# A gated linear attention kernel with a feed-forward layer: order of the constants, padded first keys and queries, a new planner table

## The chip, the cores and the metric

The kernel runs on one core of a Trainium2 chip. The metric is the device time of one execution in microseconds (us). One core has five engines with a queue of instructions each: PE (TensorE: matmuls, with weight loads beside them), ACT (ScalarE), DVE (VectorE), POOL (GpSimd) and SP (SyncE, which here only issues DMA transfers). Each engine works through its queue strictly in order; an instruction that waits holds all that stand behind it on that engine.

## The reference

Gated linear attention over 4 batches, 8 heads, 768 tokens and head dimension 48, then one feed-forward layer over the 3072 tokens with 384 features and 2048 hidden features:

```python
for t in range(S):                       # S = 768
    state = alpha[:, :, t, :, None] * state + einsum('bhd,bhe->bhde', k[:, :, t], v[:, :, t])
    y[:, :, t] = einsum('bhd,bhde->bhe', q[:, :, t], state)
x = y.transpose(0, 2, 1, 3).reshape(3072, 384)
h = x @ w_in                             # 384 x 2048
g = where(h >= 1, h, where(h <= -1, 0, (h + 1) ** 2 / 4))
out = g @ w_out                          # 2048 x 384
```

## The kernel before

**Tiles.** The tokens are cut into 24 chunks j of 128 tokens (one batch, all eight heads each, four chunks to a step in time). Three chunks make a group of 384 tokens, and the feed-forward layer runs group by group (eight groups), each over 16 steps f of 128 hidden features.

**Attention.** `prepare(j)` loads a chunk's alpha (`raw_a`, L448), keys and queries (`raw_kq`, two transfers of 48 rows, L452), values (`vt`, L464) and values again by half chunks (`both`, two transfers of 64 rows, L472). `raw_a`, `raw_kq` and `both` have two buffers that chunks use in turn, and `vt` two as well, so a load waits until the chunk two before it is done with the buffer. DVE then runs a scan (L489), a reciprocal (L493), a second scan (L496) and the multiplications of keys (L504) and queries (L521). PE transposes the keys (L541), ACT copies them (L544), PE makes scores (L556) and the state's update (L569), and `follow` masks the scores (DVE L670; for early chunks a part by ACT L642 and POOL L652), makes the shifted copy of the queries (`other`: ACT L634, or a DMA for late chunks), and grows the state (ACT L609 for the first chunk of a batch, DVE L615, L707) and places it (ACT L597, or a DMA for j >= BYDMA). PE multiplies out the chunk (L731), and `end_chunk` writes it into `xs`: for group 0 one ACT copy (L759), for later groups an ACT copy (L765), a DVE subtraction (L770) that leaves the low part, and, after a group's last chunk, six SP transfers within `xs` (L786).

**Feed-forward layer.** `hidden` multiplies x by w_in (L835 for group 0, whole fp32; L844 for the others, three products of high and low parts), ACT and DVE apply the activation (L875 twice, L885), for the split groups ACT and DVE cut the result in high and low parts (L894, L895), and `second` multiplies by w_out (L917 for group 0, L926 for the others). The products of `hidden` go to two PSUM buffers, which DVE's L885 sets free.

**Weights.** They arrive as 64-bit words, eight blocks u each of w_in and w_out (L420, 768 KB a transfer), and `decode` makes fp32 of them: ACT L344 and L352, DVE L360, L371 and L383. Group 0 takes the decoded weights; for the groups behind it `part_w` makes the high part (ACT L389), the negated high part (ACT L392), and the low part by a POOL transfer that adds the weights to it (L397). The buffers of the weights (`wt`) are shared by raw words and parts.

**Order.** A planner in Python (`Plan.order`) puts all these into one order for all engines before the kernel is built. Every operation has a cost in us and a key (a due time); at each step the planner takes the engine that can start first, and on it, among the operations that could start within NEAR of the first, the one with the lowest key. The numbers of the table at L29 to L52 shift these keys: FETCH, FETCH0 and LOAD say how long ahead of use weights and chunks are fetched, DECODE and DECODE0 how long ahead weights are decoded, PARTED when the parts are made, MARGIN and its kin how far attention runs ahead of the layer that uses it; MERGE says from which chunk PE takes update, scores and the preceding chunk's outputs in one `burst`; HELP up to which chunk ACT and POOL take masks; BYSUM, BYDMA as above and in the change. Where the planner sees PE idle before WARMTH us it adds products of zeros (`fill`, L977).

**Ends.** Before the plan stand constants (L244 to L273). After it, PE, DVE and SP add up a flag (L1006 to L1021), and every engine branches on it around `stepwise`, a slow fallback that these inputs do not need. In names of the rows below a number behind a name is a buffer's.

Of the kernel before, what the change touches and what calls it, by code (L numbers as in the profile page):

```python
# [8 lines left out]
F32 = mybir.dt.float32  # L9
# [32 lines left out]
AHEAD = 20  # L42
FIRST = 3
ROOM = 2
LATER = 4.5
MERGE = 4
WARMTH = 110
HELP = 9
BYSUM = 0
LATE = 9.5  # L50
BYDMA = 14
NEAR = 0  # L52
# [23 lines left out]
class Plan:  # L76
# [23 lines left out]
    def op(self, engine, us, key, emit, reads=(), writes=(), port=False, mode=None, moved=0, after=(), beside=False, other=None, ends=None):  # L100
        o = Op(engine, us, key, emit, port, mode, moved)
        o.ends = ends or mode
# [31 lines left out]
    def order(self):  # L134
        free = {"PE": 1.1, "DVE": 3.2, "ACT": 2.2, "POOL": 5.0, "SP": 0.8}
# [15 lines left out]
        while any(ready.values()):  # L151
# [48 lines left out]
            if o.moved > 0:  # L200
                wire = max(wire, t) + o.moved / self.RATE
                t = max(wire, t + self.LAND)
            else:
                t += self.HOP.get(o.engine, 0.08)
# [26 lines left out]
def gated_attention_ffn(ctx: ExitStack, tc: tile.TileContext, q, k, v, alpha, w_in, w_out, by, out):  # L231
# [12 lines left out]
    zeros = const.tile([P, P], BF16, name="zeros")  # L244
    nc.vector.memset(zeros, 0.0)
    nothing = zeros[:, None, :].broadcast_to([P, 2, P])
    ST = CH + 1
    raw_a = const.tile([P, 2, G * ST + 1], F32, name="raw_a")
    raw_kq = const.tile([P, 2, 2, G, CH], F32, name="raw_kq")
    for i in range(2):  # L250
        nc.vector.memset(raw_kq[:, i], 0.0)
    fwd = const.tile([P, G, ST], F32, name="fwd")
    nc.gpsimd.memset(fwd, FLOOR)
    nc.gpsimd.memset(fwd[:, :, 0], 1.0)  # L254
    bwd = const.tile([P, G, ST], F32, name="bwd")
    nc.gpsimd.memset(bwd, FLOOR_INV)
    ident = const.tile([P, P], F32, name="ident")
    make_identity(nc, ident)

    mask = const.tile([P, P], F32, name="mask")  # L260
    nc.gpsimd.memset(mask, 1.0)
    nc.gpsimd.affine_select(
        out=mask, in_=mask, compare_op=ALU.is_ge, fill=0.0, base=0, pattern=[[1, P]], channel_multiplier=-1
    )

    HC = CH // 2
    both = const.tile([P, 2, 2, 2, G, 64], F32, name="both")
    for i in range(2):
        nc.gpsimd.memset(both[:, i], 0.0)
    half_b = const.tile([P, 1], F32, name="half_b")  # L270
    nc.gpsimd.memset(half_b, 0.5)
# [922 lines left out]
```

## Time and profile before

| | |
|---|---|
| device time, median of 3 runs | 516.04 us (515.94 to 517.14) |
| the profiled execution | 516.63 us |
| its span (first to last record) | 514.7 us |
| PE, DVE, ACT, POOL busy, share of the span | 97%, 65%, 60%, 7% |
| chain that ended last, PE's share | 84% |

The profiled execution has 1.93 us outside its span and lies 0.59 us above the median. Times in rows are us from the span's start. PE is nearly always busy. The places where it waits, or works on fills, are the first 32 us (the attention of the first chunks), a handover near 100 us from group 0 to group 1, and the last 6 us.

### The profile page before, as it was taken

How to read it: one execution, taken by the hardware profiler on the slowest of the kernel's cores; microseconds unless marked ns; L12 is line 12 of the kernel's file. 1: busy time of each engine (PE TensorE's matmuls, PEld its weight loads, DVE VectorE, ACT ScalarE, POOL GpSimd, SP SyncE). 2: the span in 40 equal slices, each digit the busy share in tenths (PEclk: the TensorE clock that was granted, in tenths of full speed). 3: DMA queues.
4: the chain of work that ended last, by engine and by line, in shares of the span. 5: the costliest groups of instructions: out<-in, count | busy, mean ns of one | idle time of the engine just before them, and what ended most of it. 6: DMA issues, size and time to landing. Idle time of an engine off the chain costs nothing.

```text
span 514.7 us, 11495 instructions
## 1 busy us (share of the span) xinstructions
PE 498.7 (97%) x4685; PEld 457.8 (89%) x4685; DVE 334.2 (65%) x590; ACT 307.2 (60%) x573; POOL 37.2 (7%) x71
## 2 busy tenths in 40 slices
PE   7889999989999999999999999999999999999995
PEld 5765656579999999999999999999999999999994
DVE  7889998877557847667467667487656545343332
ACT  2879988879965655655453554453553554555551
POOL 6200011222200000000000000000000000000000
PEclk9999999999999999999999999999999999999998
DMA  8999976798634303233123423145123200000001
GB/s 236 288 358 331 268 181 139 156 211 180 126 86 111 114 22 89 74 83 96 43 67 85 138 68 91 56 101 152 35 55 67 96 19 15 16 14 34 1 2 52
DMA packets 33757, 56.08 MB, mean 109 GB/s; under 512 B 12352, under 2 KB 20512, under 8 KB 33696
## 3 DMA queue, kind: packets, MB, share of 16 engines
q1 hardware_dynamic: 31392, 48.97, 34.1%
q0 software_dynamic: 2304, 6.29, 6.8%
q8 instruction: 39, 0.64, 0.5%
q14 instruction: 22, 0.18, 0.1%
HBM read 39.38 MB, written 4.72 MB: 86 GB/s over the span
## 4 chain that ended last, share of the span: by engine, by line
PE 84%; ACT 4%; DMA 4%; issue 3%; DVE 2%; POOL 1%; SPq 1%; POOLq 0%
PE ps L926 35%; PE ps L844 34%; PE ps L731 5%; DMA wt<-wt 3%; PE ps L569 2%; PE ps L556 2%; PE ps L835 2%; PE ps L541 2%; PE ps L917 1%; PE ps L977 1%; DMA xs<-xs 1%; ACT wt L352 1%; ACT gf L875 1%; ACT w L344 1%; SPq L786 1%
## 5 line engine op out<-in xcount | busy, mean ns | idle before, releaser
L844 PE MATMUL ps<-xs,wt 128*128 128x384 f32 x1008 | 194.0, 337 | 2.2 <-DMA xs<-xs 2.2
L926 PE MATMUL ps<-gh,wt 128*128 128x384 f32 x1008 | 195.9, 340 | 0.0
L844 PEld LDWEIGHTS ps<-xs,wt 128*128 128x128 f32 x1008 | 175.9, 188 | 4.1 <-issue 2.7
L926 PEld LDWEIGHTS ps<-gh,wt 128*128 128x128 f32 x1008 | 177.1, 188 | 0.6 <-issue 0.2
L885 DVE SCALAR_TENSOR_TENSOR gf<-gf,ps 128x384 f32<-128x384 f32 x128 | 70.3, 550 | 87.7 <-ACT gf L875 87.0
L875 ACT ACTIVATE gf<-ps,half_b 128x384 f32<-128x384 f32 x128 | 74.3, 580 | 77.8 <-PE ps L844 76.3
L894 ACT CAST gh<-gf 128x384 fp32r<-128x384 f32 x112 | 57.2, 512 | 73.6 <-DVE gf L885 57.8
L895 DVE TENSOR_TENSOR gh<-gf,gh 128x384 fp32r<-128x384 f32 x112 | 62.0, 555 | 48.8 <-ACT gh L894 48.2
L875 ACT ACTIVATE gf<-gf 128x384 f32<-128x384 f32 x128 | 67.3, 526 | 3.6
L917 PE MATMUL ps<-gf,wt 128*128 128x384 f32 x96 | 33.1, 489 | 1.0 <-DVE gf L885 1.0
L835 PE MATMUL ps<-xs,wt 128*128 128x384 f32 x96 | 33.1, 489 | 0.0
L496 DVE TENSOR_TENSOR_SCAN inv<-raw_a,bwd 128x516 f32<-128x516 f32 x24 | 29.6, 1232 | 2.1
L489 DVE TENSOR_TENSOR_SCAN pre<-raw_a,fwd 128x516 f32<-128x516 f32 x24 | 29.6, 1232 | 1.7 <-POOL fwd L254 1.5
L512 POOL COPY meet<-inv 128x4 f32<-128x4 f32 x24 | 11.5, 480 | 262.2 <-DVE inv L496 262.2
L917 PEld LDWEIGHTS ps<-gf,wt 128*128 128x128 f32 x96 | 17.9, 190 | 13.4 <-DVE gf L885 1.7
L835 PEld LDWEIGHTS ps<-xs,wt 128*128 128x128 f32 x96 | 17.8, 190 | 11.3
L670 DVE TENSOR_TENSOR Q<-ps,mask 64x256 f32<-64x256 f32 x48 | 20.3, 423 | 11.2 <-DMA other<-Q 6.0
L731 PE MATMUL ps<-other,both 128*64 128x64 f32 x372 | 26.8, 225 | 0.0
L731 PE MATMUL ps<-Q,both 128*64 128x64 f32 x372 | 26.8, 225 | 0.0
L731 PEld LDWEIGHTS ps<-Q,both 128*64 128x64 f32 x372 | 23.5, 138 | 2.6 <-DVE w L360 0.5
L731 PEld LDWEIGHTS ps<-other,both 128*64 128x64 f32 x372 | 23.5, 138 | 0.0
L765 ACT CAST xs<-ps 128x512 fp32r<-128x512 f32 x21 | 12.3, 588 | 18.6 <-PE ps L731 18.4
(61 smaller groups left out, 395.0 us busy)
## 6 DMA issues: line engine op xcount, KB each, us to landing
raw_kq<-in_kq SPq DMA_DIRECT2D x48, 192.0 KB, 3.9
raw_a<-in_al SPq DMA_DIRECT2D x24, 258.5 KB, 3.4
both<-in_vb SPq DMA_DIRECT2D x48, 128.0 KB, 2.9
wt<-in_w_in SPq DMA_DIRECT2D x8, 768.0 KB, 9.2
wt<-in_w_out SPq DMA_DIRECT2D x8, 768.0 KB, 9.9
wt<-wt POOLq DMA_DIRECT2D x16, 384.0 KB, 4.9
vt<-in_vt SPq DMA_DIRECT2D x24, 192.0 KB, 3.8
out<-ot SPq DMA_DIRECT2D x24, 192.0 KB, 2.0
```

The costliest lines, as they stand in the source:

```text
L489: lambda: nc.vector.tensor_tensor_scan(flat(pre()), a[:, 0:n], flat(fwd), 0.0, ALU.mult, ALU.max),
L496: lambda: nc.vector.tensor_tensor_scan(flat(inv())[:, ::-1], a[:, 1 : n + 1][:, ::-1], flat(bwd)[:, ::-1], 0.0, ALU.mult, ALU.max),
L670: lambda r=r, u=u, to=to: nc.vector.tensor_tensor(out=to()[halves[1 - r], :, halves[u]], in0=ss(j, r)[halves[u]], in1=mask[halves[u], None ...
L731: nc.tensor.matmul(out=ps()[halves[r], to, halves[u]], lhsT=lhsT[:, u, r], rhs=x()[:, g, halves[u]], start=m + u == 0, stop=True, skip_gro ...
L835: nc.tensor.matmul(out=h(), lhsT=raw_in(f)[:, kt], rhs=whole_x(n)[:, kt].rearrange("p j t -> p (j t)"), start=kt == 0, stop=kt == KT - 1,)
L844: nc.tensor.matmul(out=h(), lhsT=win(f, w)[:, kt], rhs=xs[n]()[:, 0 : groups[n], kt, a], start=(m == 0), stop=(m == 3 * KT - 1),)
L875: lambda: nc.scalar.activation(out=gf(), in_=in_(), func=func, scale=scale, bias=bias),
L885: lambda: nc.vector.scalar_tensor_tensor(out=gf(), in0=gf(), scalar=1.0, in1=h(), op0=ALU.min, op1=ALU.max),
L894: plan.op("ACT", 0.08 + 0.41 * w, key + 0.4, lambda: nc.scalar.copy(out=gh()[:, 0], in_=gf()), [gf], [gh])
L895: sub = lambda e: e.tensor_tensor(out=gh()[:, 1], in0=gf(), in1=gh()[:, 0].bitcast(F32), op=ALU.subtract)
L917: nc.tensor.matmul(out=o_ps[seg][m](), lhsT=raw_out(f)[:, m * P : (m + 1) * P], rhs=gh(), start=f == f0, stop=f == f1 - 1,)
L926: nc.tensor.matmul(out=o_ps[seg][m](), lhsT=wout(f, w)[:, m * P : (m + 1) * P], rhs=gh()[:, a], start=(f == f0 and i == 0), stop=(f == f1 ...
```

## The change

The constants are written in a fixed order (`tc.manual_schedule()`), the keys and queries of the first two chunks come as one transfer of 128 rows each with zeros for the pads (`in_kq0`, 512 KB), instead of DVE memsets and two transfers of 48 rows (192 KB each). ACT's copy of the state (L609 before, L613 after) stands behind the first two masks of its chunk and may no longer go to DVE. The planner's table has new values. The condition on BYSUM is turned round: for weight blocks u below 7 the low part comes by POOL's transfer as before, for u = 7 by a DVE subtraction. The fallback's six loops of 128 steps become one of 768, and it writes its result through another buffer.

```diff
-FETCH = 11
-LOAD = 4.5
+FETCH = 5
+LOAD = 7.5
-PARTED = 7.0
-PREPARE = 2.5
-MARGIN = 8.0
-MARGIN0 = 14.0
-MARGIN1 = 7.0
-FETCH0 = 11
-DECODE0 = 1
+PARTED = 4.5
+PREPARE = 2.0
+MARGIN = 9.0
+MARGIN0 = 15.0
+MARGIN1 = 9.0
+FETCH0 = 6
+DECODE0 = 8.0
...
-MERGE = 4
-WARMTH = 110
-HELP = 9
-BYSUM = 0
-LATE = 9.5
-BYDMA = 14
+MERGE = 3
+WARMTH = 40
+ONCE = 7.0
+SOON = 6.0
+HELP = 7
+BYSUM = 7
+LATE = 11.5
+BYDMA = 23
...
-    for i in range(2):
-        nc.vector.memset(raw_kq[:, i], 0.0)
-    nc.gpsimd.memset(fwd, FLOOR)
-    nc.gpsimd.memset(fwd[:, :, 0], 1.0)
...
+    with tc.manual_schedule():
+        nc.vector.memset(zeros, 0.0)
+        nc.vector.memset(fwd[:, :, 0:1], 1.0)
+        nc.gpsimd.memset(fwd[:, :, 1:], FLOOR)
+        nc.gpsimd.memset(bwd, FLOOR_INV)
+        make_identity(nc, ident)
+        nc.gpsimd.memset(both[:, 0], 0.0)
...
-            if u >= BYSUM:
+            if u < BYSUM:
...
+            if j < 2:
+                load(
+                    at,
+                    lambda: nc.sync.dma_start(out=raw_kq[:, i].rearrange("p x g t -> p (x g t)"), in_=kq0[j]),
...
-                    other=("DVE", 0.33, lambda: nc.vector.tensor_copy(out=state[:, b], in_=up(j, 0)), False),
+                    after=after,
...
-                    key - 0.1,
+                    key - SOON,
                     lambda: nc.sync.dma_start(out=other()[HC:], in_=Q()[HC:]),
...
-        for c in range(S // P):
-            with tc.For_i(0, P, 1) as t:
+        with tc.For_i(0, S, 1) as t:
```

Three places show how the order moves. The first is SP, from the first block of w_in on. Before (`wt_384` is the first block of w_out, `wt_158`, `wt_256` and `wt_471` are blocks of w_in, `in_al` is alpha):

```order
L420 DMA wt_158<-in_w_in 128x768
L452 DMA raw_kq_61<-in_kq 48x1024 x2
L464 DMA vt_249<-in_vt 128x384
L420 DMA wt_256<-in_w_in 128x768
L448 DMA raw_a_60<-in_al 128x517
L472 DMA both_77<-in_vb 64x512 x2
L452 DMA raw_kq_61<-in_kq 48x1024 x2
L420 DMA wt_384<-in_w_out 128x768
L464 DMA vt_461<-in_vt 128x384
L472 DMA both_77<-in_vb 64x512 x2
L420 DMA wt_471<-in_w_in 128x768
```

After (`wt_471` is the first block of w_out, `wt_377` the second of w_in; the first of w_in stands two rows ahead of this piece):

```order
L477 DMA both_65<-in_vb 64x512 x2
L450 DMA raw_kq_60<-in_kq 48x1024 x2
L469 DMA vt_346<-in_vt 128x384
L446 DMA raw_a_59<-in_al 128x517
L418 DMA wt_377<-in_w_in 128x768
L450 DMA raw_kq_60<-in_kq 48x1024
L477 DMA both_65<-in_vb 64x512 x2
L450 DMA raw_kq_60<-in_kq 48x1024
L469 DMA vt_467<-in_vt 128x384
L418 DMA wt_471<-in_w_out 128x768
```

The first block of w_out now stands behind alpha, keys, queries and values of chunk 4 (`vt_467` is chunk 4's), before it stood behind those of chunk 3 without their values.

The second place is ACT, round the first activations of group 0 (`gf`). Before (`wt_384` and `w_647` belong to the first block of w_out, whose L352 stands five rows ahead of this piece, `wt_471` to the third of w_in):

```order
L642 COPY other_583<-ps_549 64x4x64 x2
L609 COPY state_84<-ps_546 128x192
L597 COPY both_77<-state_84 48x4x48 x2
L344 ACTIVATE w_604<-wt_471 128x768
L875 ACTIVATE gf_608<-ps_586,half_b_80 128x384
L875 ACTIVATE gf_608<-gf_608 128x384
L352 ACTIVATE wt_471<-wt_471 128x768
L875 ACTIVATE gf_634<-ps_600,half_b_80 128x384
L765 CAST xs_641<-ps_615 128x4x128
L875 ACTIVATE gf_634<-gf_634 128x384
L344 ACTIVATE w_647<-wt_384 128x768
```

After (`wt_471` and `w_598` belong to the first block of w_out):

```order
L548 COPY ks_567<-ps_540 128x512
L638 COPY other_575<-Q_536 64x512
L601 COPY both_65<-state_85 48x4x48
L389 ACTIVATE wt_534<-wt_534 128x768
L341 ACTIVATE w_598<-wt_471 128x768
L349 ACTIVATE wt_471<-wt_471 128x768
L647 COPY other_575<-ps_550 64x4x64 x2
L880 ACTIVATE gf_614<-ps_570,half_b_66 128x384
L880 ACTIVATE gf_614<-gf_614 128x384
L880 ACTIVATE gf_619<-ps_603,half_b_66 128x384
L880 ACTIVATE gf_619<-gf_619 128x384
```

Both ACT steps of the first block of w_out have come to stand ahead of the first `gf`, where one of them stood behind two pairs of `gf`; the state's copy has left the place ahead of the first `gf` and now follows the second pair.

The third place is ACT at the handover from group 0 to group 1, up to the copy that writes group 1's last chunk (`xs`, from PSUM buffer 1127 before, 1125 after). Before:

```order
L392 ACTIVATE wt_1039<-wt_1039 128x768
L544 COPY ks_1086<-ps_1074 128x512
L875 ACTIVATE gf_1089<-ps_1041,half_b_80 128x384
L875 ACTIVATE gf_1089<-gf_1089 128x384
L389 CAST wt_1144<-wt_591 128x768
L392 ACTIVATE wt_1144<-wt_1144 128x768
L389 CAST wt_1150<-wt_610 128x768
L634 COPY other_1158<-Q_1066 64x512
L765 CAST xs_641<-ps_1127 128x4x128
L642 COPY other_1158<-ps_1096 64x4x64 x2
```

After:

```order
L389 ACTIVATE wt_1023<-wt_1023 128x768
L386 CAST wt_1066<-wt_622 128x768
L880 ACTIVATE gf_1079<-ps_1047,half_b_66 128x384
L548 COPY ks_1086<-ps_1074 128x512
L880 ACTIVATE gf_1079<-gf_1079 128x384
L389 ACTIVATE wt_1066<-wt_1066 128x768
L386 CAST wt_1146<-wt_655 128x768
L638 COPY other_1154<-Q_1064 64x512
L770 CAST xs_753<-ps_1125 128x4x128
L647 COPY other_1154<-ps_1094 64x4x64 x2
```

Between the copy of keys (`ks`) and the copy to `xs` stand one CAST to a part of the weights and one negation (ACTIVATE `wt`) now, where there were two CASTs and one negation.

## Rows read from the trace of the kernel before

**Rows 1.** Windows: length, busy per engine (PE, PEld, DVE, ACT, POOL), clock, DMA share, GB/s.

```profile
5.00:10.00 5.00, 3.21 (x28) 2.38 (x26) 4.90 (x8) 0.00 (x0) 2.19 (x2) 1.00 1.05 244
30.00:40.00 10.00, 9.01 (x87) 5.83 (x88) 8.23 (x15) 8.08 (x16) 0.66 (x1) 1.00 1.04 352
32.00:100.00 68.00, 68.00 (x485) 41.95 (x485) 61.80 (x95) 61.47 (x103) 9.49 (x13) 1.00 0.86 235
110.00:500.00 390.00, 390.00 (x3617) 382.25 (x3617) 234.14 (x436) 218.98 (x421) 13.43 (x26) 1.00 0.29 73
```

**Rows 2.** Chain in order of time up to 110 us: start, length, what.

```profile
23.44 0.55 PE ps L569 x21
...
29.41 1.58 issue
...
31.80 4.07 PE ps L835 x12
35.87 1.08 PE ps L731 x32
36.95 6.00 PE ps L835 x18
```

**Rows 3.** Timeline of DVE, first scan: start, length, operation, idle before and its releaser.

```profile
4.70 1.37 DVE L489 TENSOR_TENSOR_SCAN pre<-raw_a,fwd 128x516 f32<-128x516 f32 x1 [1.53 <-POOL fwd L254]
```

**Rows 4.** First block of w_out: its issue on SP, and its KB and us to landing.

```profile
18.43 0.41 SPq L420 DMA_DIRECT2D wt<-in_w_out  x1
```

```profile
wt<-in_w_out SPq DMA_DIRECT2D x1, 768.0 KB, 9.3
```

**Rows 5.** Groups by line and shape, ACT and DVE: busy, mean ns, idle before.

```profile
L344 ACT ACTIVATE w<-wt 128x768 f32<-128x768 f32 x16 | 14.6, 913 | 1.1 <-DMA wt<-in_w_in 1.1
L597 ACT COPY both<-state 48x192 f32<-48x192 f32 x48 | 16.7, 348 | 0.8
L360 DVE TENSOR_SCALAR w<-w 128x768 int32<-128x768 int32 x16 | 8.9, 554 | 0.0
L371 DVE SCALAR_TENSOR_TENSOR w<-wt,w 128x768 int32<-128x768 int32 x16 | 15.3, 958 | 0.5
L383 DVE CUSTOM_DVE_ANT_0 wt<-wt,w 128x1536 uint16<-128x1536 uint16 x16 | 15.4, 960 | 0.6
L670 DVE TENSOR_TENSOR Q<-ps,mask 64x256 f32<-64x256 f32 x48 | 20.3, 423 | 11.2 <-DMA other<-Q 6.0 <-ACT state L609 1.8 <-ACT other L634 1.4
L885 DVE SCALAR_TENSOR_TENSOR gf<-gf,ps 128x384 f32<-128x384 f32 x128 | 70.3, 550 | 87.7 <-ACT gf L875 87.0
```

**Rows 6.** Timeline of PE at the handover, from the end of a burst on.

```profile
94.52 6.07 PE L917 MATMUL ps<-gf,wt 128*128 128x384 f32 x18
101.64 1.56 PE L917 MATMUL ps<-gf,wt 128*128 128x384 f32 x4 [1.04 <-DVE gf L885]
...
106.42 0.76 PE L844 MATMUL ps<-xs,wt 128*128 128x384 f32 x3 [2.16 <-DMA xs<-xs]
```

**Rows 7.** Timeline of ACT there.

```profile
95.54 0.83 ACT L389 CAST wt<-wt 128x768 fp32r<-128x768 f32 x1 [1.21 <-DMA wt<-wt]
96.40 0.61 ACT L634 COPY other<-Q 64x512 f32<-64x512 f32 x1
97.04 0.58 ACT L765 CAST xs<-ps 128x512 fp32r<-128x512 f32 x1
```

**Rows 8.** SP's issues of the transfers within `xs`, and the chain's last of them to its landing.

```profile
98.37 3.95 SPq L786 DMA_DIRECT2D xs<-xs  x6
```

```profile
101.72 4.56 DMA xs<-xs
```

**Rows 9.** DMA issues over the whole run: KB each, median us to landing.

```profile
xs<-xs SPq DMA_DIRECT2D x42, 48.0 KB, 2.2
```

```profile
wt<-wt POOLq DMA_DIRECT2D x16, 384.0 KB, 4.9
```

**Rows 10.** Timeline of SP, last output transfers.

```profile
508.00 1.53 SPq L965 DMA_DIRECT2D out<-ot  x3
```

More of the change, by code (lines that the diff above doesn't have):

```diff
@@ L98, in pool, with op @@
         self.sizes[name] = bufs, share or name, first or bufs
-    def op(self, engine, us, key, emit, reads=(), writes=(), port=False, mode=None, moved=0, after=(), beside=False, other=None, ends=None):
+    def op(self, engine, us, key, emit, reads=(), writes=(), port=False, mode=None, moved=0, after=(), beside=False, other=None, ends=None, land=None):
         o = Op(engine, us, key, emit, port, mode, moved)
+        o.land = land or self.LAND
         o.ends = ends or mode
@@ L134, in order @@
     def order(self):
-        free = {"PE": 1.1, "DVE": 3.2, "ACT": 2.2, "POOL": 5.0, "SP": 0.8}
+        free = {"PE": 1.1, "DVE": 1.2, "ACT": 2.2, "POOL": 4.5, "SP": 0.8}
         slots = {name: [(0.0, -i, None) for i in range(n)] for name, (n, share, _) in self.sizes.items() if share == name}
@@ L268, in gated_attention_ffn @@
[L268 to L271, printed above, removed]
-    ones = const.tile([P, 1], F32, name="ones")
-    nc.gpsimd.memset(ones, 1.0)
+    ST, HC = CH + 1, CH // 2
+    one = lambda name, shape, dt=F32: const.tile(shape, dt, name=name)
+    zeros = one("zeros", [P, P], BF16)
+    raw_a = one("raw_a", [P, 2, G * ST + 1])
+    raw_kq = one("raw_kq", [P, 2, 2, G, CH])
+    fwd, bwd = one("fwd", [P, G, ST]), one("bwd", [P, G, ST])
@@ new lines, in gated_attention_ffn @@
+    ident, mask = one("ident", [P, P]), one("mask", [P, P])
+    both = one("both", [P, 2, 2, 2, G, 64])
+    half_b, ones = one("half_b", [P, 1]), one("ones", [P, 1])
+    nothing = zeros[:, None, :].broadcast_to([P, 2, P])
+    with tc.manual_schedule():
[5 more added lines that the diff above has]
+        nc.gpsimd.memset(both[:, 0], 0.0)
+        nc.gpsimd.memset(mask, 1.0)
+        nc.gpsimd.affine_select(
+            out=mask, in_=mask, compare_op=ALU.is_ge, fill=0.0, base=0, pattern=[[1, P]], channel_multiplier=-1
+        )
+        nc.gpsimd.memset(both[:, 1], 0.0)
+        nc.gpsimd.memset(half_b, 0.5)
+        nc.gpsimd.memset(ones, 1.0)
@@ new lines, in stepwise @@
+            nc.vector.tensor_tensor(out=st, in0=st, in1=cols["a"], op=ALU.mult)
+            nc.vector.tensor_tensor(out=vr, in0=vr, in1=cols["k"], op=ALU.mult)
+            nc.vector.tensor_tensor(out=st, in0=st, in1=vr, op=ALU.add)
+            nc.vector.tensor_tensor(out=vr, in0=st, in1=cols["q"], op=ALU.mult)
+            yr = sb.tile([1, BH * D], F32, name="yr")
+            for z in range(NZ):
+                y = ps.tile([1, 512], F32, name="y")
+                nc.tensor.matmul(
+                    out=y,
+                    lhsT=ones[0:D],
+                    rhs=vr.rearrange("d n e -> d (n e)")[:, z * 512 : (z + 1) * 512],
+                    start=True,
+                    stop=True,
+                )
+                nc.vector.tensor_copy(out=yr[:, z * 512 : (z + 1) * 512], in_=y)
@@ L1139, in stepwise @@
                 nc.vector.tensor_copy(out=ot[:, m], in_=o[m])
-            nc.sync.dma_start(out=out.rearrange("(m p) t -> p m t", p=P)[:, :, bass.ds(r, P)], in_=ot)
+            nc.sync.dma_start(out=whole.rearrange("(m p) t -> p m t", p=P)[:, :, bass.ds(r, P)], in_=ot)
+        for b in range(B):
+            nc.sync.dma_start(
+                out=out.rearrange("m (c b t) -> m b c t", b=B, t=P)[:, b],
+                in_=whole.rearrange("m (b c t) -> m b c t", b=B, t=P)[:, b],
+            )
 _INS = ["q", "k", "v", "alpha"]
```

109 lines of the change are left out of this document (43 added, 66 removed).

## The prediction

> **What bounds the kernel now.** I read the windows of the long middle first: from 110 to 500 us PE is busy for 390.00 of 390.00 us, ACT for 219 and DVE for 234, the granted clock is 1.00 and DMA stands at 0.29 [rows 1]. There the products are the time, and the change takes none of them away; what ACT, DVE, POOL or SP gain or lose in this stretch is hidden as long as nobody makes PE wait. Group 0's stretch, 32 to 100 us, has PE at 68.00 of 68.00 as well, but with little beside it that is free: DVE 61.80, ACT 61.47, DMA 0.86. So time can be had or lost in three places alone. I then read the chain up to 110 us: it shows when group 0's products start (L835 at 31.80, the third step's at 36.95) and what stands ahead of them [rows 2]. The timeline of PE at the handover shows two waits, 1.04 us for the activation and 2.16 us for the transfers within `xs` [rows 6]; between the end of the burst at 94.52 and the first product of group 1 that needs those transfers, at 106.42, lie 11.90 us, of which 3.20 are these waits and 8.70 are work. The last place is the tail: the last output is issued until 509.53 [rows 10], the span ends at 514.7, and 1.93 us lie outside it.
>
> **Constants, padded keys, state copy.** The first scan waits 1.53 us for POOL's memset of a column of `fwd` [rows 3]. DVE now sets this column itself and has no memsets of `raw_kq` ahead of it, so the scan can start up to 1.5 us sooner, and the first chunk's keys are not behind four 48-row transfers any more. Pads cost 256 KB in all; from the windows' 244 and 352 GB/s [rows 1] that is 0.7 to 1.1 us of wire. But a sooner first chunk pays only if group 0's products also start sooner, and those need the first block of w_in decoded, with the steps of three chunks mixed in on ACT and DVE. Before, 1.58 us of "issue" on PE itself end 0.8 us ahead of L835 [rows 2]. I put the start of the first product at about 30 us, between 29.4 (all of that issue time gone, sooner chunks) and 31.8 (nothing gained). The state copy behind the masks takes away up to 1.8 us of DVE's waits (L670 waiting for L609) [rows 5]; by itself nothing, since it is the same chain.
>
> Of the issue time, the row shows PE without work for 1.58 us while its operands wait for nothing [rows 2]. The Trainium skill, page "Runtime: NRT & Kernel Launch", section "Instruction fetch mechanics", says that crossing to the next block of an engine's instructions is "mostly hidden"; if this stall is such a crossing, the row disagrees by 1.58 us with the DMA engines at 1.04 of their share. By the rule the sum below would be the same, less a stall that could come back.
>
> **The first block of w_out.** This is the cost. Before, it is issued at 18.43 and lands 9.3 us later, at 27.7 [rows 4], well ahead of use. Now SP has it behind chunk 4's loads. The values of chunk 4 take the buffer of chunk 2, which PE's update of chunk 2 sets free; that began at 23.44 before [rows 2], and with chunks up to 1.5 us sooner I put its end at 22 to 24. So the issue is at 22.3 to 24.0, and with 9.3 us the landing at 31.6 to 33.3. A second way by bytes, from the shapes in SP's order: ahead of it stand now alpha 5 x 258.5 KB, two transfers of 512, six of 192 for keys, five of 192 for values, eight of 128 and two blocks of 768, with itself 7.8 MB in place of 6.2; 1.5 MB more at 352 or 244 GB/s [rows 1] is 4.5 to 6.3 us, so 32.2 to 34.0. Both hold the same delay, so they are not added. I take 32.0, near the first way's lower half, because the transfers now start sooner and more of them have 128 rows.
>
> What waits for it: ACT has both its decode steps of this block ahead of the first `gf`, and DVE has all three of its steps and two masks ahead of its own step of that `gf`. PE can make steps 0 and 1 of group 0, then both PSUM buffers are taken until DVE is through. From landing on that is 0.91 + 0.55 + 0.96 + 0.96 + 2 x 0.42 + 0.55 = 4.77 us [rows 5], so step 2 starts at 32.0 + 4.8 = 36.8. Before, it starts at 36.95, with 1.08 us of outputs (L731) done that now come later [rows 2]: at like work, 35.87. Loss: **+0.9 us**. Ends: without the wait PE would come to step 2 at 29.4 + 4.07 + 0.55 = 34.0, which is -1.9; with landing at 34.0 it is +2.9.
>
> **The handover.** Before, ACT stands in L389 until 95.54, waiting 1.21 us for a POOL transfer of low parts, then makes `other` (0.61), and only at 97.04 copies the burst's result to `xs` [rows 7], 2.5 us after the burst's end. Behind this stand DVE's L770, six SP issues (3.95 us from 98.37) and a landing of 4.56 [rows 8], and the `gf` for which PE waits 1.04. Now there is one CAST fewer on the way. The one that is left (L386 of `wt_1146`) waits for the transfer two ahead (of `wt_1023`), whose negation stands ahead of the keys' copy rather than of this piece's end. So the copy to `xs` begins between 0 (the CAST is held as long as before) and 2.4 us sooner (only the burst's end binds). The landing can also come down from 4.56 towards the run's median of 2.2, and the chain need only be done 8.70 us after the burst: 0.1 to 2.5 for the copy's start, 1.3 for copy and subtraction, 3.4 to the last issue, 2.2 to 4.6 for landing is 7.0 to 11.8 [rows 7 to 9]. So between all and nothing of the 3.2 us is saved. I take the copy at +0.7 and the landing at 3.4, which gives 8.8, nearly all hidden, and keep half a us for the `gf`: **-2.6 us** (0 to -3.2).
>
> **Tail and fallback.** Fewer instructions of the fallback lie to be jumped over; the nearest row to such a jump is the issue time of 1.58 [rows 2], so 0 to -1.6, and I take **-0.3**. The page and section named above say that a taken branch to code outside the loaded blocks stops for a fetch; no run here shows whether this branch is one.
>
> **Costed at nothing.** Chunks 14 to 22 lose DMA placements to ACT: nine chunks with four copies of 0.35 and one of 0.61 [rows 5, 7], 18 us of ACT between 310 and 450 us, under PE at 100%, with ACT at 56% [rows 1]. If that cover were gone, PE would wait for `gf` by single steps of 0.5 us. The last two low parts on DVE cost two steps of about 0.96 and free two ACT steps of 0.8 and two POOL transfers of 4.9 [rows 5, 7, 9], in group 1, where DVE has room. SP's earlier query transfers and three more fills (91 to 94) hold nothing that PE waits for, as far as the rows go.
>
> **Sum.** 0.9 - 2.6 - 0.3 = -2.0 on the profiled 516.63, so 514.6 there; the median lies 0.59 lower, which makes 514.0.
>
> **Rivals.** (B) The handover does not move: ACT is still held by the POOL transfer, or SP's six issues and a landing of 4.56 take the place of that wait. For it: each of SP, POOL and ACT is near full there, and DMA at 0.86 [rows 1]. Then 0.9 - 0.3 gives 516.6, no change; with some 1 us saved, 515.6. (C) **Slower**: the first block of w_out lands late. From landing on, every us is PE time; the loss is landing less 31.1. Against a saving of 2.9 it makes the kernel slower by over 0.3% (1.55 us) from a landing at 35.6, against a saving of 1.0 at the handover from 33.6, which the count by bytes reaches. At 34.5 with 1.0 saved: 3.4 - 1.0, 518.4. (D) The landing is hidden anyway: chunk 2's update comes before 21, the block lands at 30, and step 2 waits for PE alone. Then -1 at the front, -3.2 and -0.3: 511.5. (E) The edit does not do what it says: the first scan waits for alpha rather than for `fwd`, and the chunks are no sooner; the update of chunk 2 then stays at 24.0, which is the landing of 33.3 and +2.2 in place of 0.9, so 515.3.
>
> **How the numbers follow.** A measurement of this kernel can tell some 0.3% from no change, 1.55 us: faster is below 514.49, slower above 517.59. Chances: the forecast with its neighbours within 1.3 us 0.43, of which 0.31 faster and 0.12 within the bounds; D 0.17, faster; B 0.17 and E 0.07, within the bounds; C 0.16, of which all is counted slower. Faster 0.48, same 0.36, slower 0.16. The range goes from 511.2, just past D, to 517.6, which leaves most of C out above.
>
> **What would show it.** In the trace after: the first block of w_out lands at 31 to 34 us, and the third step of L840 starts within 0.3 us of that plus 4.8 (right), or PE shows no wait ahead of it (D). At the handover the copy L770 starts within 1.4 us after the burst's end, and PE waits for `xs` less than 1 us (right), or about 2 or more (B). From the handover to 500 us PE stays at 100%; a stretch with less would make the costs at nothing wrong. The time from the last issue of an output to the span's end shows the tail.

## The result

The changed kernel takes 512.27 us at the median of 10 runs (509.38 to 518.14), the kernel before beside it 516.73 (514.8 to 517.86, 10 runs): a ratio of 0.9901, 95% interval 0.9874 to 0.9928, so about 5.1 us faster (4.5 by the medians). (Ratios, here and below, leave out disturbed executions, here one of the ten; medians do not.) The prediction was 514.0 for the median, with a range from 511.2 to 517.6, and 514.6 for the profiled execution. The profiled execution took 510.89 with a span of 509.2, before 516.63 with 514.7: 5.5 us of span to explain.

Cut at two points that both kernels have, the end of group 0's burst of attention outputs (94.52 before [rows 6], 94.46 after) and the end of the last product (508.45 before, 504.78 after), they are:

| stretch | before | after | difference | forecast |
|---|---|---|---|---|
| start to end of the burst | 94.52 | 94.46 | -0.06 | +0.9 |
| burst to last product | 413.93 | 410.32 | -3.61, of it waits at the handover -3.20 | -2.6 |
| last product to end of span | 6.25 | 4.42 | -1.83 | -0.3 |

The sum has the right sign and two of its three terms came out larger, while the loss at the front did not come. All three terms erred the same way, so the profiled execution lies 3.7 us under the forecast for it.

### The profile page after: what moved, and what is told of

Read it like the earlier page. It is cut to its first block, busy times and chain, and to the rows that moved or that the text cites. A ratio compares the mean times of both kernels' runs of the same rounds, so it can differ in the third digit from the quotient of the medians.

```text
span 509.2 us, 11489 instructions
## 1 busy us (share of the span) xinstructions
PE 498.2 (98%) x4688; PEld 457.8 (90%) x4688; DVE 331.4 (65%) x584; ACT 326.3 (64%) x623; POOL 36.0 (7%) x66
## 4 chain that ended last, share of the span: by engine, by line
PE 85%; DMA 7%; ACT 4%; issue 3%; SPq 0%; POOL 0%; DVE 0%; POOLq 0%
PE ps L931 32%; PE ps L849 31%; PE ps L840 6%; PE ps L922 6%; PE ps L736 4%; DMA wt<-in_w_in 3%; PE ps L573 2%; DMA wt<-wt 2%; PE ps L560 2%; DMA vt<-in_vt 2%; PE ps L545 1%; ACT gf L880 1%; ACT wt L389 1%; ACT gh L899 1%; ACT wt L386 1%
## 5 line engine op out<-in xcount | busy, mean ns | idle before, releaser
L840 PE MATMUL ps<-xs,wt 128*128 128x384 f32 x96 | 33.3, 491 | 0.7 <-ACT xs L764 0.7
L922 PE MATMUL ps<-gf,wt 128*128 128x384 f32 x96 | 33.2, 487 | 0.0
L601 ACT COPY both<-state 48x192 f32<-48x192 f32 x84 | 29.3, 349 | 1.3
L840 PEld LDWEIGHTS ps<-xs,wt 128*128 128x128 f32 x96 | 17.7, 190 | 12.6 <-ACT xs L764 0.8
L922 PEld LDWEIGHTS ps<-gf,wt 128*128 128x128 f32 x96 | 17.9, 190 | 11.7
```

What stands on the lines that cost most here:

```text
L601: lambda r=r, to=to: nc.scalar.copy(out=to, in_=state[low[r], b]),
L840: nc.tensor.matmul(out=h(), lhsT=raw_in(f)[:, kt], rhs=whole_x(n)[:, kt].rearrange("p j t -> p (j t)"), start=kt == 0, stop=kt == KT - 1,)
L922: nc.tensor.matmul(out=o_ps[seg][m](), lhsT=raw_out(f)[:, m * P : (m + 1) * P], rhs=gh(), start=f == f0, stop=f == f1 - 1,)
```

## The profile after

The changed kernel's windows, in the columns of [rows 1]: length, busy time of PE, PEld, DVE, ACT and POOL, granted clock, DMA share, GB/s.

```profile
32.00:100.00 68.00, 68.00 (x515) 41.97 (x514) 63.30 (x97) 61.08 (x105) 9.53 (x12) 1.00 0.85 245
110.00:500.00 390.00, 389.76 (x3534) 382.64 (x3534) 231.75 (x427) 239.84 (x472) 10.99 (x22) 1.00 0.25 65
```

The long middle is as full as before: what was costed at nothing cost nothing. ACT has 21 us more in it (239.84 for 218.98), which is the 18 us of copies in chunks 14 to 22 and some more, and PE waits 0.24 us in all.

The front: DVE's first scan, PE's first update and then its rows from the first product of group 0 on, DVE's step on the first two `gf`, and the issue and landing of the first block of w_out (SP's row, then KB and us to landing).

```profile
3.60 1.23 DVE L493 TENSOR_TENSOR_SCAN pre<-raw_a,fwd 128x516 f32<-128x516 f32 x1 [2.58 <-DMA raw_a<-in_al]
```

```profile
10.48 0.68 PE L573 MATMUL ps<-vt,ks 64*64 64x48 f32 x32 [1.97 <-DMA vt<-in_vt]
...
30.89 2.20 PE L840 MATMUL ps<-xs,wt 128*128 128x384 f32 x6 [0.67 <-ACT xs L764]
33.03 0.68 PE L573 MATMUL ps<-vt,ks 64*64 64x48 f32 x32
33.64 6.07 PE L840 MATMUL ps<-xs,wt 128*128 128x384 f32 x18
39.55 2.10 PE L922 MATMUL ps<-gf,wt 128*128 128x384 f32 x6
```

```profile
38.00 1.02 DVE L890 SCALAR_TENSOR_TENSOR gf<-gf,ps 128x384 f32<-128x384 f32 x2
```

```profile
24.70 0.42 SPq L418 DMA_DIRECT2D wt<-in_w_out  x1
```

```profile
wt<-in_w_out SPq DMA_DIRECT2D x1, 768.0 KB, 8.3
```

The scan is 1.1 us sooner than in [rows 3], although it now waits for alpha, the sign that rival E named. The gain does not last: PE waits 1.97 us for the values of chunk 0, which land later (issued at 2.69 they take 7.7 us; before, issued at 1.27, they took 2.8). The first product starts at 30.89, and ends a wait for ACT's copy L764, which stands behind the decode of a block of w_in that landed at 28.0. The block of w_out lands at 24.70 + 8.3 = 33.0, and PE waits for it nowhere.

The handover, PE's rows from the burst on, then ACT, SP and POOL there, to be laid beside [rows 6 to 8]; the last row is the time from issue to landing of the six transfers.

```profile
94.46 7.36 PE L922 MATMUL ps<-gf,wt 128*128 128x384 f32 x22
101.36 3.66 PE L849 MATMUL ps<-xs,wt 128*128 128x384 f32 x18
```

```profile
94.11 0.83 ACT L386 CAST wt<-wt 128x768 fp32r<-128x768 f32 x1 [1.88 <-DMA wt<-wt]
94.96 0.62 ACT L638 COPY other<-Q 64x512 f32<-64x512 f32 x1
95.60 0.58 ACT L770 CAST xs<-ps 128x512 fp32r<-128x512 f32 x1
```

```profile
94.55 1.12 SPq L477 DMA_DIRECT2D both<-in_vb  x2
95.72 0.58 SPq L469 DMA_DIRECT2D vt<-in_vt  x1
96.94 3.96 SPq L791 DMA_DIRECT2D xs<-xs  x6
```

```profile
92.53 0.84 POOL L394 DMA_DIRECT2D wt<-wt  x1 [2.54 <-ACT wt L389]
...
100.48 0.87 POOL L394 DMA_DIRECT2D wt<-wt  x1 [2.87 <-ACT wt L389]
```

```profile
DMA to landing us min/median/max: 2.2/2.2/2.5
```

No wait is left in PE's rows. ACT's copy starts at 95.60 instead of 97.04, SP's first issue at 96.94 instead of 98.37, and the slowest landing is 2.5 instead of 4.6. POOL's transfer, which was issued before the last of the six (at 101.72 [rows 8]),

```profile
101.19 0.86 POOL L397 DMA_DIRECT2D wt<-wt  x1 [1.79 <-ACT wt L392]
```

now comes 0.2 us behind it: 100.48 to 100.3.

The tail is the chain's last pieces:

```profile
501.58 3.20 PE ps L931 x17
504.78 0.02 issue
504.80 0.56 DVE ot L322
```

From 504.78 to 509.2 are 4.42 us. In the kernel before the last product ends at 508.45,

```profile
505.25 3.20 PE ps L926 x17
```

and the span at 514.7.

## Experiments

All times are medians, the ratio is to runs of the kernel before on the same chip with its 95% interval. Two kernels come from exchanging one part (the fallback), two from doing one part alone, and eight from moving single steps in the finished order: `moved_behind(order, steps, anchor)` takes the named steps, and whatever depends on them or follows them on their engine among those held, to just behind the anchor.

**The tail: the fallback alone, and the change without it.** Kernel before with the short fallback; kernel after with the long one.

```diff
-        for c in range(S // P):
-            with tc.For_i(0, P, 1) as t:
+        with tc.For_i(0, S, 1) as t:
```

> The kernel before with the short fallback alone. Theory (tail): the fallback's length is what an engine jumps over at the end, so the time from the last product to the span's end falls from 6.25 us (before) to about 4.4 us (the whole change shows 4.42), all else is as before, and the time falls by 1.8 us, ratio 0.9965. Rival: the shorter tail comes from where the last outputs land or from where instructions lie after the reordering; then the tail stays at about 6.2 us and the ratio is 1.000.

> The changed kernel with the long fallback of before put back. Theory (tail): from the last product to the span's end about 6.2 us again, 1.8 us more than with the whole change (4.42), so about 3.6 us under the kernel before in the profile, ratio 0.993 to 0.994. Rival (tail from another part of the change): 4.4 us, ratio 0.990.

Measured: 515.1 us, 0.9961 (0.9931 to 0.999), for the short fallback alone; 514.66, 0.9914 (0.9883 to 0.9945), for the change without it. In the traces the chain of the first ends

```profile
506.78 3.20 PE ps L926 x17
509.98 0.02 issue
```

of a span of 514.5: 4.5 us to the end. In the second it ends at 503.85 of 509.9, which leaves 6.05:

```profile
500.65 3.20 PE ps L931 x17
```

The short loop takes 1.6 to 1.7 us off the end, in either kernel. All fourteen profiles of this document part the same way: from the last product to the end are 5.96 to 6.40 us in the eight kernels with the long fallback and 4.38 to 4.79 in the six with the short one. A jump over the code would explain why code that no run enters costs time there, but the runs show the size alone, not which instruction takes it.

**The rest by halves.** First the planner's numbers, the condition on BYSUM and the earlier query transfers, on the kernel before; then the constants, the padded keys and the state copy, on the kernel before.

```diff
-BYSUM = 0
+BYSUM = 7
...
-            if u >= BYSUM:
+            if u < BYSUM:
```

> The kernel before with the new table alone (with the turned condition on BYSUM, the earlier query transfers and the landing time that the planner takes for the low parts), old constants, old first loads, old fallback. Theory (the handover is the table's): PE waits under 0.5 us in all at the handover from group 0 to group 1, where before waits 1.04 + 2.16; the tail stays at 6.2 us; the first product of group 0 starts within 1 us of before (31.8). Time 2.5 to 3.5 us under before, ratio 0.993 to 0.995. Rival (the handover came from the earlier front, since PE's burst ends at the same time in both): PE still waits 2 us or more there, ratio 0.999 to 1.000.

```diff
+    with tc.manual_schedule():
+        nc.vector.memset(zeros, 0.0)
+        nc.vector.memset(fwd[:, :, 0:1], 1.0)
...
+            if j < 2:
+                load(
```

> The kernel before with the order of the constants, the padded first keys and queries, and the state copy behind the masks alone; old table, old fallback. Theory (the sooner scan is lost to the transfers): the first scan starts at 3.6 us in place of 4.7, but the first product of group 0 starts at most 1 us sooner than before (31.8), since the weights and values of the first chunks share one full wire; what the time gains beside that, 0 to 3 us, is the handover, which this order also changes (one step of the parts between the copy of the keys and the copy to xs in place of two). Rival (the front carries through): the first product starts 1.5 to 2.5 us sooner and the burst before the handover ends as much sooner than 94.5.

Measured: 519.98, 1.0062 (1.003 to 1.0095), slower; and 517.88, 1.0013 (0.999 to 1.0037), no change. Neither half clears the wait for `xs`: PE waits 2.4 us in the first and 2.2 in the second. The wait of 1.04 for the activation is gone in the first, and three products of zeros stand there in the second; from the burst's end to the product that needs the last `xs` are 10.85 and 11.01 us, where there were 11.90. PE's first product starts at 31.73 and 31.39, against 31.80 before, but with the table alone the burst ends at 97.33, 2.8 us later than before, which is more than it gains. So the end of the wait for `xs` belongs to the order that both make together.

**What held the copy to `xs`.** The prediction said: ACT's CAST ahead of it. So that one CAST goes behind the copy, in the kernel before; and in a second kernel the negation in front of it too, which takes POOL's transfer along.

```diff
-            for o in plan.order():
+            for o in moved_behind(plan.order(), [tags["cast", 2, "o"]], tags["xs", 5]):
```

> The kernel before with one step of ACT moved: the CAST that stood ahead of the copy to xs at the handover (95.54 in the trace of before) goes behind it. All other engines keep their order. Theory of the prediction (ACT is what is late): the copy to xs begins 1.4 to 2.4 us sooner and PE's waits there fall from 3.2 us to under 1, time 2.5 us down, ratio 0.995. Theory formed since (SP is late as well: its two loads ahead of the transfers within xs take 3.6 us in place of 1.7 while a transfer issued by POOL runs beside them): the copy is sooner, but the first transfer within xs is still issued at about 98.3, 3.8 us after the burst, and PE's waits stay at 2.5 to 3.2 us in all, ratio 0.999 to 1.001.

> The kernel before with two steps of ACT moved behind the copy to xs at the handover: the same CAST, and the negation ahead of it, after which POOL issues a transfer of low parts (at 94.63 in the trace of before, just when SP begins the two loads ahead of the transfers within xs). Theory (SP beside a POOL transfer): with no such transfer there, SP's two loads take about 1.7 us, the first transfer within xs is issued 2 us after the burst's end in place of 3.9, and PE's waits at the handover fall from 3.2 us to under 0.5; time 2.7 to 3.2 us down, more where a wait also took the clock, ratio 0.993 to 0.995. Theory of the prediction (ACT alone): the same as the run with the CAST alone moved, whatever that shows.

Measured: 518.46, 1.0018 (0.9994 to 1.0043), and 516.33, 0.9984 (0.9954 to 1.0014): no change in either. The trace of the first, ACT, SP, POOL, then PE:

```profile
95.07 0.59 ACT L765 CAST xs<-ps 128x512 fp32r<-128x512 f32 x1 [0.28 <-PE ps L731]
```

```profile
95.02 2.26 SPq L472 DMA_DIRECT2D both<-in_vb  x2
97.33 0.58 SPq L464 DMA_DIRECT2D vt<-in_vt  x1
98.00 4.96 SPq L786 DMA_DIRECT2D xs<-xs  x6
```

```profile
99.96 0.86 POOL L397 DMA_DIRECT2D wt<-wt  x1 [1.58 <-ACT wt L392]
```

```profile
103.69 0.76 PE L844 MATMUL ps<-xs,wt 128*128 128x384 f32 x3 [0.88 <-DMA xs<-xs]
106.42 3.78 PE L844 MATMUL ps<-xs,wt 128*128 128x384 f32 x12 [1.98 <-DMA xs<-xs]
```

The copy is 2.0 us sooner, as asked for, and the first issue only 0.37 (the burst ends at 94.92 here, 0.4 later), because SP still has the values of the next chunk in hand until 97.91. POOL's transfer has come forward as well, to 99.96, into the midst of the six issues. PE waits 2.9 us for `xs`, where it waited 2.16; the 1.04 for the activation is gone. ACT alone was not what bound.

In the second, POOL has no transfer beside SP's loads: these take 2.13 us (1.55 and 0.58) in place of 3.57, and the first issue comes 2.36 us after the burst's end in place of 3.85. But POOL's transfers are now issued at 97.63 and 101.50, and the six land in 2.2 to 4.6 us. PE waits for them as long as ever:

```profile
106.60 2.35 PE L844 MATMUL ps<-xs,wt 128*128 128x384 f32 x12 [2.28 <-DMA xs<-xs]
```

So an early ACT and an early SP together do not clear the wait either.

**POOL's transfer out of the way.** If the 384 KB transfer of low parts is what makes the six land late, a kernel in which it is issued behind them must land them in 2.2. In the kernel before, two negations and their POOL transfers go behind the copies of an output (`ot`); then the same with the CAST moved as well.

```diff
-            for o in plan.order():
+            for o in moved_behind(plan.order(), [tags["neg", 2, "o"], tags["low", 2, "o"], tags["neg", 4, "i"], tags["low", 4, "i"]], tags["ot", 0, 1]):
```

> The kernel before with two negations of ACT at the handover, and the two POOL transfers of low parts behind them (issued at 101.19 and 102.79 in the trace of before), moved behind ACT's copies of group 0's output; nothing else. Theory (a POOL transfer that is issued ahead of SP's last transfers within xs holds their landing): the last transfer within xs lands in 2.2 to 2.6 us in place of 4.56, PE's wait of 2.16 us for it falls to under 0.4, its wait of 1.04 for the activation stays; time 1.8 to 2.2 us down and another 1 to 2 us in executions in which the wait took the clock, ratio 0.992 to 0.997. Theory of the prediction (ACT's late copy to xs alone): no change, PE waits 3.2 us in all.

> The same two transfers moved, and the CAST moved behind the copy to xs as well. Theory: both waits of PE at the handover are under 0.5 us; 2.7 to 3.2 us under before in the profile, ratio 0.990 to 0.995, so the handover of the changed kernel is had by these orders alone. Rival (SP's two slow loads ahead of the transfers within xs still hold them): PE waits 0.5 to 1.5 us for xs.

Measured: 521.42, 1.0077 (1.0049 to 1.0105), and 520.67, 1.0063 (1.0036 to 1.0091), both slower. Yet the wait for `xs` is gone in the first, where the six land in

```profile
DMA to landing us min/median/max: 2.2/2.2/2.7
```

and nearly gone in the second:

```profile
102.45 3.39 PE L844 MATMUL ps<-xs,wt 128*128 128x384 f32 x18 [0.18 <-DMA xs<-xs]
```

The first one's PE, then ACT, then the windows after:

```profile
100.72 1.56 PE L917 MATMUL ps<-gf,wt 128*128 128x384 f32 x4 [0.90 <-DVE gf L885]
101.82 3.63 PE L844 MATMUL ps<-xs,wt 128*128 128x384 f32 x18
...
114.94 1.11 PE L569 MATMUL ps<-vt,ks 64*64 64x48 f32 x32 [5.24 <-ACT ks L544]
```

```profile
110.38 0.83 ACT L389 CAST wt<-wt 128x768 fp32r<-128x768 f32 x1 [5.97 <-DMA wt<-wt]
```

```profile
112.00:115.00 3.00, 0.06 (x4) 0.06 (x5) 2.12 (x5) 2.97 (x7) 1.04 (x2) 0.50 0.16 33
115.00:118.00 3.00, 3.00 (x86) 2.88 (x88) 2.14 (x6) 3.00 (x6) 0.00 (x0) 0.50 0.79 177
```

The late transfers keep ACT's next CAST waiting for 5.97 us, the keys of the next chunk (`ks`, L544) stand behind that CAST, and PE waits 5.24 us for them (4.09 in the second kernel); then the granted clock is 0.50, the lower level of 1.2 GHz, for three us of work. The theory on the landing holds, and the price of moving the transfer by itself is larger than the wait it removes.

**The kernel after, with single steps moved.** Chunk 0's values ahead of chunk 1's loads; the copy L764 ahead of the decode in front of it; the POOL transfer behind the copies of an output; and all three.

```diff
-            for o in plan.order():
+            for o in moved_behind(plan.order(), [tags["load", 1, "a"], tags["load", 1, "kq"]], tags["load", 0, "vt"]):
```

> The changed kernel with the values of chunk 0 issued ahead of alpha, keys and queries of chunk 1; SP's order alone, by that one move. Theory (the sooner scan is lost to chunk 0's values, which land at 10.3 us behind 1.5 MB): PE's wait of 1.97 us ahead of the first L573 falls to under 0.7, the masks of chunk 0 come 1 to 1.5 us sooner, chunk 1 may lose up to 1 us; the first product of group 0 starts 0 to 1 us sooner than 30.9, since it waits for ACT behind the second block of w_in, and the time falls by 0 to 1 us. Rival (the values set the front): the first product starts 1.5 to 2 us sooner and the time falls by as much.

```diff
-            for o in plan.order():
+            for o in moved_behind(plan.order(), [tags["decode", 1, "i", 1], tags["decode", 1, "i", 2], tags["cast", 0, "i"]], tags["xs", 2]):
```

> The changed kernel with three steps of ACT (both decode steps of the second block of w_in, and the first CAST to a part) moved behind the copy to xs of chunk 2; ACT's order alone. Theory (the first product stands behind a decode that it doesn't need): the copy begins at about 28.0 in place of 30.37, PE's wait ahead of L840 (0.67) is gone and the first product starts 0.6 to 0.7 us sooner, held then by chunk 3's scores; the later decode costs nothing, as the second block is first needed by step 2. Time 0.6 us down, below what can be told. Rival (the decode is on the path of step 2): PE waits 0.5 to 1.5 us between steps 1 and 2 and the gain is gone.

```diff
-            for o in plan.order():
+            for o in moved_behind(plan.order(), [tags["neg", 3, "i"], tags["low", 3, "i"]], tags["ot", 0, 1]):
```

> The changed kernel with one negation of ACT at the handover, and the POOL transfer of low parts that follows it, moved behind ACT's two copies of group 0's output; every other order is kept. The transfer is the one that POOL issues at 100.48 in the trace of the changed kernel, 0.2 us after SP's last transfer within xs began its issue (landing 2.5 us); in the run with the copy to xs ahead of the decode it was issued at 100.00, ahead of the last one, which then took 5.1 us to land, and PE waited 2.77 us. Theory (who of the two comes first decides, and it is a matter of tenths of a us): with the transfer out of the way the last one lands in 2.2 to 2.5 us every time, PE never waits at the handover, the profile stays at 509 to 510 us, and the runs lose their upper half: median 0.5 to 1.5 us below the changed kernel's, ratio 0.986 to 0.989. Rival (the spread of the changed kernel is the front's): the same median as the changed kernel, ratio 0.990.

> The changed kernel with three moves: values of chunk 0 ahead of chunk 1's loads, copy to xs of chunk 2 ahead of the second block's decode, and the transfer of low parts behind the output's copies. Theory (first product held by ACT behind the second block of w_in, and by chunk 0's values ahead of that): the first product starts at 28.0 to 29.3 in place of 30.9, and PE then waits 0.3 to 1.5 us for the first block of w_out at the first L922, since that lands at 33 us as before; the burst before the handover ends 0.5 to 1.5 us sooner than 94.5, no wait at the handover; profile 507.5 to 508.7 us, ratio 0.982 to 0.986. Rival (the first block of w_out sets the end of the front): the burst ends at 94.0 to 94.5 and the time is that of the run with the transfer moved alone.

Measured, in this order: 511.37, 0.9871 (0.982 to 0.9922); 512.22, 0.9892 (0.9843 to 0.9941); 511.97, 0.9902 (0.9864 to 0.9939); 512.21, 0.9874 (0.9838 to 0.9909). All intervals overlap that of the change itself, 0.9874 to 0.9928: no version beats it by what these runs can tell. With the values first, PE's wait for them is gone and the first chunk's update is 1.9 us sooner (8.59 for 10.48), but the first product starts at 30.02 only, after 1.60 us of waiting for the copy L764, and its six products then take 3.73 us instead of 2.20, at a granted clock of 0.64 and 0.51 in the windows from 30 to 34 us. With the copy ahead of the decode it starts at 29.86 without a wait, one us sooner than in the change, but 0.30 and 0.40 us of waits by 42 us give the lead back: the second six products of L922 start at 42.05, in the change at 41.92. The transfer behind the outputs leaves the median where it was, although its expectation had it 0.5 to 1.5 us lower. With all three moves the first product starts at 30.79 and the burst ends at 95.56; the expected 28.0 to 29.3 and the profile of 507.5 to 508.7 (it took 513.12) did not come. At the handover the kernel with the copy ahead of the decode shows what the change rests on:

```profile
101.34 1.52 PE L849 MATMUL ps<-xs,wt 128*128 128x384 f32 x6
105.63 2.32 PE L849 MATMUL ps<-xs,wt 128*128 128x384 f32 x12 [2.77 <-DMA xs<-xs]
```

```profile
100.00 0.87 POOL L394 DMA_DIRECT2D wt<-wt  x1 [2.87 <-ACT wt L389]
```

```profile
DMA to landing us min/median/max: 2.2/2.2/5.1
```

The order there is that of the change; POOL's transfer is issued at 100.00 and SP's last `xs` at 100.4, where the change has 100.48 and 100.3. With that the landing is 5.1 and the wait is back.

**All the traces side by side.** The start of the last of the six issues (the view of the tile `xs`), the start of the last POOL transfer that was issued within 1.5 us ahead of it, or else of the nearest, the slowest landing of the six and PE's wait for `xs`, of the one profiled execution of each kernel:

| kernel | last `xs` issue | POOL's transfer | slowest landing | PE waits for `xs` |
|---|---|---|---|---|
| before | 101.7 | 101.19 | 4.6 | 2.2 |
| short fallback alone | 101.8 | 101.00 | 4.7 | 2.5 |
| table alone | 103.6 | 103.34 | 4.4 | 2.4 |
| front alone | 101.9 | 100.86 | 4.4 | 2.2 |
| CAST behind `xs` | 101.4 | 99.96 | 4.9 | 2.9 |
| CAST and transfer behind `xs` | 102.3 | 101.50 | 4.6 | 2.3 |
| copy before decode | 100.4 | 100.00 | 5.1 | 2.8 |
| after | 100.3 | 100.48 | 2.5 | 0 |
| after, long fallback | 99.5 | 99.70 | 2.4 | 0 |
| values first | 100.9 | 100.88 | 2.8 | 0 |
| transfer behind outputs | 98.5 | 101.45 | 2.9 | 0 |
| three moves | 101.7 | 104.48 | 2.4 | 0 |
| before, transfers late | 100.8 | 103.97 | 2.7 | 0 |
| before, both | 100.8 | 103.95 | 4.7 | 0.2 |

In each of the seven kernels that have POOL's transfer issued 0.3 to 1.4 us ahead of the last `xs`, this last one takes 3.9 to 5.1 us to land and PE waits 2.2 us or more. In the other seven POOL's transfer is issued at the same time or later, the last `xs` lands in 2.2 to 2.4, and PE waits at most 0.2 us; the slowest landing is that of the first of the six there. The 4.7 in the last row is such a first one, issued at 97.44, 3.0 us behind a POOL transfer of 94.43; PE's 0.18 us end with the first two. From one to the next the landing falls to 2.2 us, so the last is in at about 103.0.

## Why the prediction held, step by step

**Front, +0.9: wrong.** The landing was right (33.0 for 32.0, in the range of 31.6 to 34.0), in part by luck: the issue at 24.70 was later than the 22.3 to 24.0 expected, and the 8.3 us to landing shorter than the 9.3. The path behind it was right too: 33.0 + 4.77 gives 37.8 for DVE's step on the first `gf`, and it begins at 38.00. The step that failed was "then both PSUM buffers are taken until DVE is through". PE's rows above have 24 products of L840, four steps, from 30.89 to 39.7 with no wait for DVE: the third began near 35.7 and the fourth near 37.7 (33.64 and six or twelve products of 0.34), while the first `gf` was through only at 38.5. The two buffers that DVE sets free are a limit of the planner alone (`bank("ps_h", 2, ...)`), which counts them while it makes the order; the tiles themselves come from one pool of eight, and PE went on. So the block of w_out is needed only by the first L922 at 39.55, and with a first `gf` at 38.5 there was about one us to spare. In the kernel with the copy ahead of the decode PE comes there one us sooner and waits 0.30: DVE ends the first `gf` there at about 38.9, and L922 starts at 38.98.

Rival D had step 2 wait for PE alone, but for another reason (a landing at 30), and put the front at -1. In the two profiled executions nothing of it is left by the end of the burst (-0.06). But these two are not all that bears on it: the long fallback and the transfer behind the outputs leave the changed front as it is, and have their first product at 29.30 and 29.11 and the burst's end at 93.59 and 92.53, where the change has 30.89 and 94.46. Five of the kernels above have the front of before, with the burst's end from 93.75 to 95.73, where it was 94.52. The means are 93.5 of three and 94.8 of six, so a gain of about one us is likelier than none; with executions of one front up to 2 us apart, so few do not settle it.

**Handover, -2.6: right in size, half right in cause.** All 3.20 us went. The copy starts 1.14 us after the burst, where 0.7 was taken, and PE waits for `xs` not at all. But the step put ACT at the root of both waits, and took the landing as a number that "can also come down from 4.56", 3.4. ACT is the root of one: the 1.04 us for the activation are gone in all three kernels of before in which the CAST moved, and 0.90 stay where it did not. Moving ACT's CAST alone gave 0.37 us at the first issue and nothing at the end. For the wait for `xs` the landing is what the runs show to bind: with ACT and SP early it kept the whole wait of 2.28, and with POOL's transfers out of the way the wait was gone although ACT and SP were as late as before (first issue 3.71 us after the burst's end, before 3.85). So POOL's next transfer must be behind the last `xs`, which then lands in 2.2 to 2.4 instead of 3.9 to 5.1.

SP counts as well, by a sum that no run shows alone. The chain has 8.70 us. In the change the last issue comes 5.8 us after the burst and lands in 2.2, which is 8.0. With the last issue of before, 7.2 us after the burst, it would be 9.4; where SP was that late and POOL out of the way, PE's other wait of 0.90 us stood ahead and covered it. The two transfers of values took 3.57 us of issue in the trace of before, where POOL's transfer is issued at 94.63, and 1.70 after, with it at 92.53:

```profile
94.62 2.28 SPq L472 DMA_DIRECT2D both<-in_vb  x2
96.95 1.29 SPq L464 DMA_DIRECT2D vt<-in_vt  x1
```

(SP of the kernel before, ahead of [rows 8].) In rival B these were "SP's six issues and a landing of 4.56", with a chance of 0.17; the change passed it by 0.2 us between two issues, which no step of the prediction had, and that is luck.

**Tail, -0.3: right in sign, mis-sized.** It is -1.8 between the two profiles and 1.6 to 1.7 by the two exchanges of the fallback, at or a little past the bound of -1.6 that was taken from PE's issue time of 1.58 [rows 2]. The value taken was far from the row that it rested on, for no reason that the rows gave.

**Costed at nothing: right.** The middle has PE at 389.76 of 390.

**From the profile to the median.** The terms above are 3.5 us off together, and all to one side; the profiled execution was forecast at 514.6, took 510.89, and lies under rival D too (512.1 for it, 511.5 for the median). The median is only 1.7 us from its forecast because it was taken 0.59 below the profiled execution, as it was for the kernel before in three runs, while in ten runs the changed kernel's lies 1.38 above its own. That 512.27 lies well within the range is in part luck.

The sum was set against one execution at a full clock. Of 71 executions of the kernel before beside these experiments, 14 had a mean granted clock of 0.995 or more, with a median of 516.46 us, and 57 a lower one, with 517.73. Of the nine of the changed kernel that its ratio counts, six were at 0.995 or more, at 510.76, and three below, at 514.86. At the higher clock the gain is 5.7 us, the same as between the two profiled executions (516.63 and 510.89). What else the wait at the handover does is seen in the kernel with the short fallback alone, in windows of two us around it (the last row is the kernel before, in the window of the second):

```profile
104.00:106.00 2.00, 0.05 (x1) 0.00 (x0) 1.83 (x4) 0.26 (x1) 0.18 (x1) 1.00 1.08 186
106.00:108.00 2.00, 1.43 (x5) 1.46 (x6) 1.23 (x1) 0.66 (x2) 0.00 (x0) 0.50 1.07 249
108.00:110.00 2.00, 2.00 (x9) 2.00 (x8) 0.93 (x2) 1.74 (x3) 0.00 (x0) 0.64 0.98 331
```

```profile
106.00:108.00 2.00, 1.58 (x9) 1.62 (x10) 1.32 (x2) 1.30 (x3) 0.00 (x0) 1.00 1.11 247
```

PE has nothing to do for two us, and most of the next three are granted at half, 1.2 GHz: five products in the second window, where the profile of before and the kernel with CAST and transfer moved had nine and eight, at 1.00, after much the same wait. The profiles of the table alone, the front alone and the moved CAST have the fall too. So a wait of about two us there costs its own length in some executions and over an us more in others. Those nine executions of the changed kernel still spread, from 509.38 to 515.57, and so does the version with the transfer moved out of the race (509.96 to 515.75); where that comes from was not shown.

**Left open.** Why neither half gives the order that clears the handover is known only by its rows, not by the numbers in the table that make it. Whether the 0.2 us between SP's last issue and POOL's transfer hold in every execution was seen in four profiles of this order and its kin (three times yes, once no).

## What to carry

A limit in a planner need not be a limit for the engines that run its order: before a wait is priced, find the buffer that the instruction really needs, and the first one that reads what is late. A transfer's time to land is not a single number with a spread; ask which big transfer is issued just ahead of it, from which engine, and by how many tenths of an us, since moving one step moves both. Code that never runs can still cost at the end: measure it by exchanging it alone. And one profiled execution of each kernel is a thin base for a term of one us: look for other kernels that share the stretch.

## What the runs showed of the hardware

The last of six 48 KB transfers from SP's queue landed in 2.2 to 2.4 us, and in 3.9 to 5.1 when a 384 KB transfer from POOL's was issued 0.3 to 1.4 us ahead of it; the first of six took 4.7 when one had been issued 3.0 us ahead. SP's own issues vary: the two of 128 KB took 1.12 us in the change, with POOL's transfer 2.0 us earlier, and 2.28 and 2.26 with it 0.0 and 0.6 us earlier (the kernel before, CAST behind `xs`). But they took 1.12 with it 0.6 us earlier too (both moves in the kernel before) and 1.55 with it 4.4 us earlier (CAST and transfer moved), so what lengthens them was not shown. A shorter program after the end of the work, in a branch that is not taken, gave back 1.6 to 1.7 us. The granted clock, in windows of two us, fell to 0.50 to 0.72 for some three us behind a wait of 2.0 to 2.5 us in the profiles of four kernels (short fallback alone, table alone, front alone, CAST behind `xs`), and stayed at 1.00 in those of three others with a wait as long (the kernel before, CAST and transfer moved, copy before decode).
